# Two fills of idle matmuls in an attention kernel's head, made in row tiles of the TensorE array

## The chip, the cores and the metric

The kernel runs on one core of a Trainium2 chip. A time is the device time of one execution in microseconds; the median over the runs is given. A profile is one execution recorded by the hardware profiler. The engines are TensorE (PE; its weight loads are shown as PEld), VectorE (DVE), ScalarE (ACT), GpSimd (POOL) and SyncE (SP), each with an instruction queue of its own, in order.

## The reference

An attention through 32 inducing points, and then a max-out layer on its result:

```python
def mab(q, kv):
    s = scale * (q @ kv.transpose(0, 2, 1))
    s = s - s.max(-1, keepdims=True)
    a = np.exp(s)
    a /= a.sum(-1, keepdims=True) + 1e-09
    return a @ kv
h = mab(I, x)          # I: (4, 32, 128), x: (4, 12544, 128)
y = mab(x, h)          # (4, 12544, 128), then seen as 50176 rows

g = np.maximum(y @ w1, y @ w2)     # w1, w2: (128, 1024)
return (g @ w_out)                 # w_out: (1024, 128)
```

All inputs and the output are float32; the kernel computes in float16 with float32 sums.

## The kernel before

The core's work falls into a head and a main part. The four batches of x have 98 blocks of 128 rows each. The head computes `h` for batch 0. The main part makes the outputs of all four batches, and beside them, spread out, `h` of the next batch.

**The order.** Each engine's instructions are written out by the program in a fixed order. A planner (`Clock`, `ck` in the code) keeps an estimated time for TensorE, ScalarE, VectorE and each of the eight banks of PSUM. `ck.run(us, mode)` moves TensorE's clock on, with an extra for a change of mode: "full" (the whole 128 x 128 array), "col" (four column tiles of 32 columns) or "row" (four row tiles of 32 rows). `ck.bank[i]` is the time at which bank i has been read out. `bank()` takes the bank with the lowest time, or the one that `only` names. These clocks choose banks, engines and order when the program is built. On the chip the engines wait for each other by semaphores, which follow from what is read and written: an instruction that writes a bank waits until the last reader of what was in it is done.

**The head.** Batch 0 comes in 11 parts, `parts[0]`, four of 14 blocks and then smaller ones. For each part TensorE

- transposes its blocks (`p1_transpose`, L232) into two banks, the first 8 of 14 into one and 6 into the other; VectorE copies the first to SBUF (L236), ScalarE the second (L239),
- accumulates the part before it (`p1_accum`): sums of the exponentials (L271) and `h` (L280), which take the result of ScalarE's exponential (L257),
- computes the scores of the part (`p1_scores`, L248) from the copied transposes into another bank, which ScalarE's exponential (L257) reads.

Two of the eight banks are kept for the accumulation of the whole head (`st[0]["hps"]`, `st[0]["eps"]`; their time is `INF`), so six are in turn.

Between these steps there are idle matmuls: `WARM` = 9 of 512 columns at the start (L665), two in the middle of part 0's transposes, and after the transposes of parts 0, 1 and 2 a `fill` of 2, 2 and 1 matmuls of 512 columns (L657). They multiply `warm`, a tile of zeros, into a bank that nobody reads. For i = 1 and 2 the step of the loop reads: transposes of part i, fill, accumulation of part i - 1, scores of part i.

**The main part.** In turns, TensorE makes phases in row tiles (L990, four units side by side, each with a bank of its own) and full matmuls against `w_out` (L809); ScalarE (L1006) and VectorE (L1009) read the phases' banks. A table `DEV` holds, by the number of the step, where the order departs from the planner's own rule. `pool_accum` (L364) works in column tiles.

Of the kernel before, what the change touches and what calls it, by code (L numbers as in the profile page):

```python
# [102 lines left out]
def kernel(  # L103
# [9 lines left out]
    nc = tc.nc  # L113
# [25 lines left out]
    ck = Clock()  # L139
    uid = [0]  # L140

    def bank(shape, dtype=F32, only=None):
        i = min(range(8), key=lambda j: ck.bank[j]) if only is None else only
        uid[0] += 1
        return i, psum.tile(shape, dtype, name=f"ps{uid[0]}", tag=f"bank{i}", bufs=1)
# [34 lines left out]
    warm = consts.tile([128, 512], F16, name="warm")  # L180
# [16 lines left out]
    with tc.manual_schedule(engines={ET.PE, ET.DVE, ET.Activation, ET.Pool, ET.SP}):  # L197
# [25 lines left out]
        def p1_transpose(b, i, between=0):  # L223
            k0, n = parts[b][i]
            xn = xn_at[b, i]
            h = min(8, (n + 2) // 2)
            for g, m in ((0, h), (h, n - h)):
                if g and between:
                    fill(between)
                bi, ps = bank([128, 8, 128], F16)  # L230
                for j in range(m):
                    nc.tensor.transpose(ps[:, j, :], xn[:, g + j, :], identity16)  # L232
                end = ck.run(0.056 * m, ready=ck.bank[bi], why="T")
                dst = xT_tiles[b % 2][:, k0 + g : k0 + g + m, :]
                if g == 0:
                    nc.vector.tensor_copy(out=dst, in_=ps[:, 0:m, :])  # L236
                    ck.bank[bi] = ck.on_dve(end, 0.08 + 0.075 * m)
                else:
                    nc.scalar.copy(out=dst, in_=ps[:, 0:m, :])  # L239
                    ck.bank[bi] = ck.on_act(end, 0.05 + 0.12 * m)  # L240
                st[b]["xT", i] = max(ck.bank[bi], st[b].get(("xT", i), 0.0))

        def p1_scores(b, i):
            k0, n = parts[b][i]
            bi, ps = bank([128, 512])
            ck.wait(max(ck.bank[bi], st[b].get(("xT", i), 0.0)), "p1")
            for j in range(n):
                nc.tensor.matmul(  # L248
                    out=ps[:, j * M : (j + 1) * M],
                    lhsT=xT_tiles[b % 2][:, k0 + j, :],  # L250
                    rhs=inducingT,
                    start=True,
                    stop=True,
                )
            end = ck.run(0.029 * n)
            et = etp.tile([128, P1, M], F16, name=f"et_{b}_{i}", tag="et")
            nc.scalar.activation(out=et[:, 0:n, :], in_=ps[:, 0 : n * M], func=AF.Exp, scale=scale)  # L257
            ck.bank[bi] = ck.on_act(end, 0.05 + n * M / 1200.0)
            st[b]["et", i] = et, ck.bank[bi]

        def p1_accum(b, i, lo=0, hi=P1):
            k0, n = parts[b][i]
            et, ready = st[b]["et", i]
            hi = min(hi, n)
            xn = xn_at[b, i]
            if b == 0:
                last = i == len(parts[0]) - 1
                ck.wait(ready, "p1")
                for j in range(lo, hi, 4):
                    m = min(4, hi - j)  # L270
                    nc.tensor.matmul(  # L271
                        out=st[0]["eps"][0 : m * M, 0:1],
                        lhsT=et[:, j : j + m, :].rearrange("p k m -> p (k m)"),
                        rhs=ones16[:, 0:1],
                        start=(i == 0 and j == 0),
                        stop=(last and j + m == n),
                        skip_group_check=True,
                    )
                for j in range(lo, hi):
                    nc.tensor.matmul(  # L280
                        out=st[0]["hps"][:, 0:M],
                        lhsT=xn[:, j, :],
                        rhs=et[:, j, :],
                        start=(i == 0 and j == 0),
                        stop=(last and j == n - 1),
                    )
                st[0]["end"] = ck.run(0.029 * (hi - lo) + 0.03 * ((hi - lo + 3) // 4))
                return
# [365 lines left out]
        def fill(n):  # L654
            bi, ps = bank([128, 512])
            for _ in range(n):
                nc.tensor.matmul(out=ps, lhsT=warm[:, 0:128], rhs=warm, start=True, stop=True)  # L657
            ck.run(0.22 * n)
# [4 lines left out]
        bi, ps = bank([128, 512])  # L663
        for _ in range(WARM):
            nc.tensor.matmul(out=ps, lhsT=warm[:, 0:128], rhs=warm, start=True, stop=True)  # L665
        for n in ("h", "e"):
            st[0][n + "b"], st[0][n + "ps"] = bank([128, 512])
            ck.bank[st[0][n + "b"]] = INF
        for i in range(4):
            p1_transpose(0, i, 2 if i == 0 else 0)  # L670
            if i < 3:
                fill(2 - i // 2)
            if i == 0:
                bi, ps = bank([128, 512])
                nc.tensor.transpose(ps[:, 0:M], ind_sb, identity32[0:M, 0:M])
                nc.vector.tensor_copy(out=inducingT, in_=ps[:, 0:M])
                ck.bank[bi] = 0.0
                nc.vector.reduce_sum(out=diag, in_=identity32.rearrange("p (k m) -> p m k", m=M), axis=AX.X)
                for dst, f in ((rep32, DOWN / scale), (repd, 1.0)):
                    nc.vector.tensor_scalar(  # L680
                        out=dst.rearrange("p (k m) -> p k m", m=M),
                        in0=diag[:, None, :].broadcast_to((128, 4, M)),
                        scalar1=f,
                        scalar2=None,
                        op0=ALU.mult,
                    )
            if i > 0:
                p1_accum(0, i - 1)
            p1_scores(0, i)
# [515 lines left out]
```

## Time and profile before

| | us |
|---|---|
| median of 2 runs | 327.43 |
| lowest and highest run | 327.39, 327.47 |
| span of the profiled execution, first to last instruction | 325.6 |
| TensorE busy in the span | 319.8 |
| VectorE busy | 283.1 |
| ScalarE busy | 281.7 |
| GpSimd busy | 25.6 |

The profiled execution has the span of 325.6 us, and some 1.8 us of the run's time lie outside it. Busy times of different engines overlap. The costliest groups are the full matmuls of the main part (L809: 3136 of 128 columns, 217.3 us busy, with overlaps between one and the next) and its phases (L990: 88.7 and 38.8 us). In views of the timeline a line gives the start, the length from the first instruction's start to the last one's end, the engine, the kernel's line, the operation, out<-in, the shape, and how many instructions were put together. A matmul of 128 columns is shown some 0.22 us long although the next one starts 0.056 us after it, because the matmuls are pipelined.

### The profile page before, as it was taken

The page shows a single profiled execution, that of the slowest core. Times are in us where ns is not written, and L with a number is a line of the kernel's source. Part 1 is how long each engine was busy: PE and PEld are TensorE (multiplying, and loading weights), DVE is VectorE, ACT ScalarE, POOL GpSimd, SP SyncE. Part 2 cuts the span into 40 slices and gives each one's busy share as a digit, 9 for nine tenths or more (in the row PEclk, how much of TensorE's full clock was granted, in tenths as well). Part 3 has the DMA queues.
Part 4 walks back from the last instruction along what each step waited for, and adds up shares of the span by engine and source line. Part 5 has one row for each costly group of instructions (what it writes and reads, how often), then busy time and mean ns, then how long its engine had stood idle before and what let it go on. Part 6 is the DMA issues. An engine that isn't in the chain of part 4 may idle for free.

```text
span 325.6 us, 12570 instructions
## 1 busy us (share of the span) xinstructions
PE 319.8 (98%) x5404; PEld 243.0 (75%) x5404; DVE 283.1 (87%) x509; ACT 281.7 (87%) x560; POOL 25.6 (8%) x51
## 2 busy tenths in 40 slices
PE   7999999999999999999999999999999999999996
PEld 3876777777767777777777777777777777778785
DVE  3359989989989998998989999998989999999973
ACT  3679899999989899998888999989969999999961
POOL 7452030000040000000040000000000000000000
PEclk9999999999999999999999999999999999999999
DMA  8999999976279999993389999992312312222233
GB/s 204 208 206 214 286 246 212 172 207 134 97 150 245 225 248 209 201 203 86 116 162 243 214 234 232 190 192 86 115 66 101 113 68 98 90 108 99 85 115 112
DMA packets 70823, 53.65 MB, mean 165 GB/s; under 512 B 52176, under 2 KB 55408, under 8 KB 70768
## 3 DMA queue, kind: packets, MB, share of 16 engines
q1 hardware_dynamic: 64656, 38.63, 49.2%
q0 software_dynamic: 6112, 14.22, 22.3%
q8 instruction: 42, 0.69, 0.9%
q14 instruction: 13, 0.11, 0.1%
HBM read 28.33 MB, written 25.69 MB: 166 GB/s over the span
## 4 chain that ended last, share of the span: by engine, by line
PE 95%; DVE 1%; DMA 1%; ACT 0%; issue 0%; ACTq 0%; DVEq 0%
PE ps L809 61%; PE ps L990 22%; PE ps L591 2%; PE ps L232 2%; PE ps L308 2%; PE ps L364 1%; DMA xf<-in_x_dram 1%; PE ps L248 1%; DVE relu L1009 1%; PE ps L280 1%; PE ps L641 1%; PE ps L766 1%; PE ps L271 1%; PE ps L657 0%; PE ps L473 0%; PE ps L409 0%
## 5 line engine op out<-in xcount | busy, mean ns | idle before, releaser
L1006 ACT ACTIVATE relu<-ps 128x512 f16<-128x512 f32 x461 | 244.8, 602 | 26.6 <-PE ps L990 18.1
L1009 DVE TENSOR_SCALAR relu<-ps 128x512 f16<-128x512 f32 x323 | 206.8, 682 | 16.9 <-PE ps L990 15.3
L809 PE MATMUL ps<-woutp,relu 128*128 128x128 f16 x3136 | 217.3, 220 | 0.0
L809 PEld LDWEIGHTS <-relu 128*128 128x128 f16 x3136 | 176.7, 98 | 39.6 <-issue 29.1
L990 PE MATMUL ps<-e,hwd 32*128 32x512 f16 (+2 forms) x880 | 88.7, 360 | 0.0
L836 DVE TENSOR_TENSOR o<-ps,rp 128x512 f32<-128x512 f32 (+3 forms) x108 | 68.5, 634 | 5.5 <-PE ps L809 3.4
L990 PEld LDWEIGHTS <-hwd 32*128 32x128 f16 x880 | 24.9, 91 | 21.1 <-issue 1.0
L990 PE MATMUL ps<-m,e 32*128 32x128 f16 x381 | 38.8, 217 | 0.0
L990 PEld LDWEIGHTS <-e 32*128 32x128 f16 x381 | 21.3, 93 | 2.6
L165 POOL DMA_DIRECT2D xn<-in_x_dram x31 | 17.0, 557 | 8.2 <-DMA xn<-in_x_dram 4.3
L236 DVE COPY xT<-ps 128x512 f16<-128x512 f16 (+3 forms) x11 | 5.5, 504 | 7.8 <-PE ps L232 7.7
L319 ACT ACTIVATE eu<-ps 128x512 f16<-128x512 f32 x18 | 10.8, 615 | 0.0
L603 ACT ACTIVATE e<-ps 128x512 f16<-128x512 f32 (+2 forms) x21 | 10.5, 577 | 0.0
L164 POOL COPY pace<-hacc 128x1 f32<-128x1 f32 x2 | 0.4, 184 | 114.8 <-DVE hacc L397 114.8
L591 PE MATMUL ps<-xT,hT 128*32 128x512 f16 (+3 forms) x114 | 8.9, 362 | 0.0
L239 ACT COPY xT<-ps 128x768 f16<-128x768 f16 (+3 forms) x11 | 6.1, 556 | 2.7 <-PE ps L232 2.6
L232 PE MATMUL ps<-identity,xn 128*128 128x128 f16 x98 | 7.4, 219 | 0.4 <-DVE xn L661 0.3
L232 PEld LDWEIGHTS <-xn 128*128 128x128 f16 x98 | 5.6, 97 | 1.6 <-DVE xn L661 1.1
L257 ACT ACTIVATE et<-ps 128x448 f16<-128x448 f32 (+4 forms) x11 | 4.5, 413 | 2.6 <-PE ps L248 2.6
L308 PE MATMUL ps<-xT,inducingT 128*32 128x512 f16 x72 | 6.5, 385 | 0.0
L591 PEld LDWEIGHTS <-hT 128*32 128x32 f16 x114 | 3.3, 94 | 4.1 <-issue 3.0
L364 PE MATMUL ps<-xn,eT 128*32 128x128 f16 x288 | 5.5, 220 | 0.0
(96 smaller groups left out, 108.2 us busy)
## 6 DMA issues: line engine op xcount, KB each, us to landing
out_dram<-o SPq DMA_DIRECT2D x90, 256.0 KB, 2.4
xn<-in_x_dram POOLq DMA_DIRECT2D x24, 448.0 KB, 11.8
out_dram<-o SPq DMA_DIRECT2D x10, 128.0 KB, 3.0
xn<-in_moe_w_dram POOLq DMA_DIRECT2D x4, 256.0 KB, 14.1
xn<-in_x_dram POOLq DMA_DIRECT2D x4, 224.0 KB, 10.2
xT<-xn SPq DMA_TRANSPOSE x42, 4.3
xf<-in_x_dram SPq DMA_DIRECT2D x1, 512.0 KB, 3.9
xf<-in_x_dram SPq DMA_DIRECT2D x1, 384.0 KB, 4.3
```

The lines of the kernel that those rows point to most:

```text
L165: nc.gpsimd.dma_start(out=xn_at[b, i][:, 0:n, :], in_=xr[b, :, k0 : k0 + n, :])
L232: nc.tensor.transpose(ps[:, j, :], xn[:, g + j, :], identity16)
L308: nc.tensor.matmul(out=ps[32 * g : 32 * (g + 1), :], lhsT=inducingT, rhs=xT_tiles[b % 2][:, U * u + 4 * g : U * u + 4 * (g + 1), :], start ...
L319: nc.scalar.activation(out=eu, in_=ps, func=AF.Exp, scale=scale, accum_out=st[b]["es"][:, u : u + 1])
L364: nc.tensor.matmul(out=ps[32 * g : 32 * (g + 1), 0:128], lhsT=eT[:, j, 32 * g : 32 * (g + 1)], rhs=xn_of(b, U * v + 4 * g + j), start=(j = ...
L591: nc.tensor.matmul(out=ps[32 * q : 32 * (q + 1), 128 * t : 128 * (t + n)], lhsT=hq, rhs=xT[:, c : c + n, :], start=True, stop=True, tile_p ...
L603: nc.scalar.activation(out=blk.e2[:, 0 : 128 * wd], in_=ps[:, 0 : 128 * wd], func=AF.Exp, scale=st[0]["rs"] if blk.b == 0 else scale,)
L809: nc.tensor.matmul(out=g.ps[:, 128 * c : 128 * (c + 1)], lhsT=g.blk.relu[q][:, 128 * (jb * w4 + t) : 128 * (jb * w4 + t + 1)], rhs=woutp[: ...
L836: nc.vector.tensor_mul(osb[:, 0:n, :], g.ps[:, 0 : n * C].rearrange("p (s c) -> p s c", s=n), rp)
L990: nc.tensor.matmul(**seq[i])
L1006: nc.scalar.activation(out=dst, in_=src, func=AF.Relu)
L1009: nc.vector.tensor_scalar(out=dst, in0=src, scalar1=0.0, scalar2=None, op0=ALU.max)
```

## The change

The fills after the transposes of parts 1 and 2 are made by a new function, `fill_rows`. The fill of part 0 stays.

`fill_rows(i)` sorts the banks by their times, takes a tile in each of the first six, and tells the planner to wait for all six. Its matmuls have 32 rows of `warm` as weights and 32 rows as data, at row tile r (rows 32r to 32r + 31), and write all 128 partitions of a bank.

- For i = 1 there are 20 rounds of four matmuls of 128 columns, row tile r into the r-th of the six banks.
- For i = 2 there are four segments. In each, a row tile has one bank, in four pieces of 128 columns; a tile marked "w4" or "w5" makes one matmul of 512 columns in the fifth or sixth bank instead. Between segments the banks go to other row tiles. Before the third segment stands an empty instruction of TensorE that waits for the last narrow matmul of the first, and before the fourth segment one that waits for the last of the second.

In all these are 80 matmuls for i = 1 and 48 for i = 2 (13, 13, 9 and 13), in place of two and one. The planner is told 1.1 and 0.8 us of mode "row".

```diff
+        marks = {}
+        NOFUSE = False
+
+        def fill_rows(i):
+            order = sorted(range(8), key=lambda j: ck.bank[j])[0:6]
+            ps6 = [bank([128, 512], only=bi)[1] for bi in order]
+            for bi in order:
+                ck.wait(ck.bank[bi], "fill")
+
+            def mm(r, k, lo, n, first):
+                rows = slice(32 * r, 32 * (r + 1))
+                return nc.tensor.matmul(
+                    out=ps6[k][:, lo : lo + n],
+                    lhsT=warm[rows, 0:128],
+                    rhs=warm[rows, 0:n],
+                    start=first,
+                    stop=True,
+                    tile_position=(32 * r, 0),
+                    skip_group_check=True,
+                )
+
+            if i == 1:
+                for v in range(20):
+                    for r in range(4):
+                        mm(r, r, 128 * (v % 4), 128, v == 0)
+            else:
+                seen = set()
+                for n, seg in enumerate(({0: 0, 1: 1, 2: 2, 3: "w4"}, {0: "w5", 1: 1, 2: 2, 3: 3}, {1: "w4", 2: 2, 3: 0}, {0: 1, 1: 3, 2: 2, 3: "w5"})):
+                    for v in range(4):
+                        for r, k in seg.items():
+                            if v == 0 and r == min(seg) and n > 1:
+                                nop = nc.tensor.nop(nofuse=NOFUSE)
+                                tc.add_manual_dep(
+                                    nop.ins,
+                                    marks[n - 2].ins.name,
+                                    mybir.DependencyInfo(mybir.DependencyClass.Sync, mybir.DependencyReason.DATA),
+                                    reason="row tiles of one bank",
+                                )
+                            if isinstance(k, int):
+                                ins = mm(r, k, 128 * v, 128, k not in seen and not seen.add(k))
+                                marks[n] = ins
+                            elif v == 0:
+                                mm(r, int(k[1]), 0, 512, True)
+            ck.run(1.1 if i == 1 else 0.8, "row")
+
         for i in range(4):
             p1_transpose(0, i, 2 if i == 0 else 0)
             if i < 3:
-                fill(2 - i // 2)
+                fill_rows(i) if i else fill(2)
             if i == 0:
```

## The prediction

> **What bounds the kernel now.** I read the page first (busy shares, clock), then the waits of TensorE alone, then the timeline of the head, where the two fills lie, and last a few phases further on, for the price of row tiles.
>
> ```profile
> span 325.6 us, 12570 instructions
> PE 319.8 (98%) x5404; PEld 243.0 (75%) x5404; DVE 283.1 (87%) x509; ACT 281.7 (87%) x560; POOL 25.6 (8%) x51
> PEclk9999999999999999999999999999999999999999
> ```
>
> TensorE is busy for 98% of the span, and no slice shows a clock below nine tenths. The windows of 5 to 24 us and of 24 to 326 us say it more exactly: granted clock 1.00 in both, TensorE busy for 17.79 of 19.00 and 298.20 of 302.00 us. There is no cold stretch that more filling could cure.
>
> ```profile
> engine line waited for: us in total, times, longest us
> PE ps L665 <- DVE warm L213: 1.2, 1, 1.2
> PE ps L232 <- DVE xn L661: 0.3, 1, 0.3
> PE ps L271 <- ACT et L257: 0.3, 1, 0.3
> PE ps L248 <- DVE inducingT L676: 0.3, 1, 0.3
> ```
>
> These are all the waits of TensorE's matmuls in the whole run. None is for a transfer; the last, that of L271, ends at 15.41 us (timeline), and from 20 us on the list is empty. So what delays TensorE in the head delays everything behind it, one for one: no later wait is there to swallow it.
>
> ```profile
> 8.37 0.94 PE L232 MATMUL ps<-identity,xn 128*128 128x128 f16 x14
> 9.14 0.60 PE L657 MATMUL ps<-warm 128*128 128x512 f16 x2
> 9.58 0.34 PE L271 MATMUL ps<-ones,et 128*128 128x1 f16 x4
> ...
> 10.56 0.94 PE L232 MATMUL ps<-identity,xn 128*128 128x128 f16 x14
> 10.75 0.54 ACT L257 ACTIVATE et<-ps 128x448 f16<-128x448 f32 x1 [0.60 <-PE ps L248]
> 11.21 0.69 DVE L236 COPY xT<-ps 128x1024 f16<-128x1024 f16 x1 [1.50 <-PE ps L232]
> ...
> 11.34 0.38 PE L657 MATMUL ps<-warm 128*128 128x512 f16 x1
> ...
> 11.54 0.80 ACT L239 COPY xT<-ps 128x768 f16<-128x768 f16 x1 [0.25 <-PE ps L232]
> 11.56 0.34 PE L271 MATMUL ps<-ones,et 128*128 128x1 f16 x4
> ```
>
> Columns: start, length, engine, line. The chunk loop runs on TensorE without a hole here: transposes (L232), fill (L657), sums (L271), accumulation (L280), scores (L248), transposes again. The fill after chunk 1 holds TensorE from 9.14 to 9.58, 0.44 us; that after chunk 2 from 11.34 to 11.56, 0.22 us.
>
> **The order of the rest does not change.** The planner's clock is told 1.1 and 0.8 us of row work, two changes of mode each, and to wait for all banks. By its own arithmetic TensorE ends chunks 1, 2, 3 at 5.10, 7.43, 9.76 before and at 6.93, 10.80, 13.13 after. At the end of chunk 3 ScalarE (10.38 to 13.75) and VectorE (8.76 to 12.12) are later by the same 3.37, and so is every bank that is still to matter. All its later choices compare differences of these clocks, so the same instructions follow in the same order, in the same banks. What is left is the real time of two fills.
>
> **Prices.** Row tiles of the phases:
>
> ```profile
> 33.93 0.39 PE L990 MATMUL ps<-e,hwd 32*128 32x512 f16 x4
> 34.26 0.90 PE L809 MATMUL ps<-woutp,relu 128*128 128x128 f16 x13
> 35.09 0.23 PE L990 MATMUL ps<-m,e 32*128 32x128 f16 x1
> ...
> 77.15 1.08 PE L364 MATMUL ps<-xn,eT 128*32 128x128 f16 x64
> ```
>
> Four 512-wide matmuls of four row tiles need 0.39 us together, as one does (385 ns in the groups): they run side by side. From their start to the first full matmul is 0.33; the columns take 0.22 of it (one fill of 512: 11.34 to 11.56), so a turn from row to full costs some 0.11. The 13 full matmuls end their columns at 34.26 + 13 x 0.056 = 34.99, and the phase starts at 35.09: 0.10 for full to row. I take 0.10 for each turn, four in all.
>
> [...]
>
> Pace of narrow matmuls, four tiles at once: no row here has four row tiles of 128 columns in a long run. The nearest is L364, four column tiles of 128 columns: (1.08 - 0.22) / 63 = 13.7 ns each, 55 ns for a round of four. The full array's 128 columns take 0.056 (14 transposes from 8.37 to 9.14). I take 0.056 a round. The other bound is the 25 ns of a full-array pair of load and matmul (L248: 14 in 0.35 us), should loads of 128 columns of weights go in one by one.
>
> **Fill 1** (after chunk 1): 20 rounds of four. It uses the four longest-free banks; the latest is that of chunk 0's scores, read by ScalarE's L257 from 8.55 to 9.09, over before 9.14. So it waits for nothing, and takes 0.10 + 20 x 0.056 + 0.10 = 1.32 us where 0.44 was: **+0.88**.
>
> **Fill 2** (after chunk 2): four segments of four rounds, 0.224 each. It takes all six free banks, the two latest as spares "w4" and "w5". These are the banks of chunk 2's own transposes, just written and still to be copied out by VectorE (L236) and ScalarE (L239). In the times of the trace of before: row work may start at 11.34 + 0.10 = 11.44. Its fourth matmul writes w4, so it waits for VectorE's copy, 11.21 + 0.69 = 11.90, and some 0.05 for the signal (ScalarE's copy of chunk 3 ends at 14.35 on the chain of waits, and TensorE goes on at 14.39). The second segment begins with w5 and waits for ScalarE's copy, 11.54 + 0.80 + 0.05 = 12.39. The first segment is over by then (11.95 + 0.224). Three segments and a turn remain: 12.39 + 3 x 0.224 + 0.10 = 13.16, where L271 began at 11.56: **+1.60**. These two waits are new. Behind them in TensorE's order stand the rest of the fill, the accumulation of chunk 1, the scores of chunk 2 and the whole head; ScalarE and VectorE wait for those. Nothing covers it, because the copies used to run beside accumulation (L280), which now comes later.
>
> **TensorE's waits on itself:** before segment 3 for a matmul of segment 1, before segment 4 for one of segment 2. The first is long past. The second ends with the last round of segment 2, started at 12.39 + 0.17, 0.22 long, plus 0.05: 12.83, just where segment 3's columns end (12.84). I take 0. Below nothing is excluded, for the wait replaces none; above, I allow 0.2 each, the longest idle time put down to issue before L990's loads.
>
> Sum: 0.88 + 1.60 = 2.48 us. The profiled execution's span of 325.6 plus 1.8 outside it is the 327.43 of the median. **Forecast: 327.43 + 2.48 = 329.9 us, 0.76% slower.** A change under 2% is about what a measurement of this kernel cannot tell from none, so this counts as the same.
>
> Low end: if the copies were over in time, fill 2 would cost 0.10 + 0.90 + 0.10 - 0.22 = 0.88 and the sum be 1.76; with 0.4 less, a tenth of the 3.8 us that TensorE is idle from 24 to 326 us, should those holes move, 328.8. High end: at 25 ns a matmul fill 1 takes 80 x 0.025 = 2.0 (0.88 more) and a segment of 13 0.33 (three of them 0.3 more): 3.66, or 331.1, and half of a self-wait's 0.2 makes it 331.2.
>
> **Rivals.**
> *The fills are hidden (0.08).* If the loads of x set the head's pace, longer fills would only take the place of waiting, and the time stay at 327.4 to 328.2. For it: the transfers are dense in the head (share 1.17 from 5 to 24 us). Against: TensorE waits for no transfer, in the list above.
>
> *Row tiles do not run side by side (0.04).* If 128-wide row matmuls went one at a time, at 56 ns, fill 1 would take 4.5 us instead of 1.12 (+3.4). Segments two and four of fill 2, 12 x 0.056 + 0.22 = 0.89, would cost 0.67 more each, the third (nine matmuls) 0.44, and the first, no longer over in its wait, 0.45. Together 5.6 on top of 2.48: 335.5 us, 2.5% slower. It decides once the extra passes 4.1 us, at about 48 ns a matmul. Against: the phases' four in 0.39.
>
> *The clock falls (0.04).* Cold fills (L665) take 3.85 / 9 = 0.43 us where warm ones take 0.22. To pass 2% the head would need 8.1 us more of work at half pace. Against: 1.00 throughout, across a stop of 0.3 us; the longest new one, for VectorE's copy, is 0.5.
>
> [...]
>
> *A faster kernel (0.02)* would need 6.5 us; all of TensorE's waits after warming sum to 0.9, so I see no source.
>
> **How the numbers follow.** My forecast has the remaining 0.82. The range, 328.8 to 331.2, takes in its ends, and leaves the rivals and a little of its own tails out. Faster by over 2%: 0.02; slower by over 2%: 0.05 (serial tiles, or most of a cold clock); within: 0.93.
>
> **What would show it.** Right: the first L271 after fill 1 some 0.88 us later than 9.58, that after fill 2 2.5 us later than 11.56; about 80 row matmuls in 1.1 us; a stop of 0.4 to 0.5 us in fill 2 put down to VectorE's L236 and a shorter one to ScalarE's L239; the rest of the head and of the span shifted by the same 2.5 us. Wrong: L271 on time, a clock below 1.00, row matmuls over 14 ns apart, or a main part whose length differs by more than 0.5 us.

## The result, and the profile after

| | before | the change |
|---|---|---|
| median, us | 327.43 (2 runs) | 332.93 (2 runs, 332.69 and 333.16) |
| ratio, 95% interval | | 1.016 [1.0123, 1.0197] |
| span of the profiled execution, us | 325.6 | 331.0 |
| granted clock, mean over the span | 1.000 | 0.995 |

The kernel became 5.5 us slower; 2.5 were forecast, with 331.2 as the end of the range. Beside thirteen other runs of the kernel before (median 327.52) four later runs of the change gave 333.33, ratio 1.0177 [1.0158, 1.0196].

From the page of the profile after, the lines that answer to those of before:

```profile
span 331.0 us, 12820 instructions
PE 324.1 (98%) x5529; PEld 246.3 (74%) x5529; DVE 283.0 (85%) x509; ACT 281.9 (85%) x560; POOL 25.5 (8%) x51
PEclk9979999999999999999999999999999999999999
```

VectorE and ScalarE do what they did. The clock line has a digit that was not there: 7 in the third slice, 16.6 to 24.8 us.

The waits of TensorE's matmuls:

```profile
PE ps L665 <- DVE warm L213: 1.2, 1, 1.2
PE ps L680 <- issue: 1.1, 1, 1.1
PE ps L248 <- DVE inducingT L721: 0.3, 1, 0.3
PE ps L680 <- DVE xT L236: 0.3, 1, 0.3
PE ps L469 <- PE ps L591: 0.3, 1, 0.3
```

L680 is the matmul of `fill_rows`. The wait for VectorE's copy was forecast. The second of the list was not: 1.1 us for "issue", that is, for nothing that the profile shows. (The last is at 28.35 us, and will come up again.) The timeline of TensorE says where:

```profile
9.92 1.30 PE L680 MATMUL ps<-warm 32*128 32x128 f16 x80
11.15 0.35 PE L271 MATMUL ps<-ones,et 128*128 128x1 f16 x4
...
13.02 0.23 PE L680 MATMUL ps<-warm 32*128 32x128 f16 x3
13.53 1.37 PE L680 MATMUL ps<-warm 32*128 32x512 f16 x38 [0.28 <-DVE xT L236]
15.96 0.34 PE L680 MATMUL ps<-warm 32*128 32x128 f16 x7 [1.06 <-issue]
16.23 0.35 PE L271 MATMUL ps<-ones,et 128*128 128x1 f16 x4
...
17.22 1.58 PE L232 MATMUL ps<-identity,xn 128*128 128x128 f16 x14
```

Fill 1 goes as forecast. Fill 2 stops in the middle of its fourth segment, six matmuls behind its last wait on itself. The sixth begins at 14.57 and the seventh at 15.96; less 0.05 for the sixth one's columns, that is a stop of 1.33 us. Then the transposes of part 3 take 1.58 us where they took 0.94: the clock has fallen. The windows show it (second column: length, then busy times of PE, PEld, DVE, ACT, POOL; behind them PEclk):

```profile
13.92:17.33 3.41, 2.30 (x69) 1.80 (x69) 0.00 (x0) 0.00 (x0) 1.97 (x3) 1.00 1.14 203
17.33:20.75 3.42, 3.42 (x56) 3.08 (x52) 0.94 (x2) 1.89 (x3) 2.12 (x4) 0.50 1.19 205
20.75:24.16 3.41, 3.39 (x85) 3.24 (x85) 1.45 (x4) 2.40 (x7) 1.27 (x3) 1.00 1.38 208
```

In the clock's own records it is at half from 17.33 to 20.75 us.

**Where 5.4 us between the two profiles come from**, by the starts of the same steps: the first scores (L248) 8.02 to 8.70, 0.68 before the change begins; L271 behind fill 1 9.58 to 11.15, 0.89 more; L271 behind fill 2 11.56 to 16.23, 3.10 more, of which 1.33 is the stop and 1.77 the fill; the transposes of part 4 14.56 to 19.88, 0.65 more, the slow window; the first phase 24.29 to 29.65, 0.04 more, and 5.4 at the end. The main part is as long as it was. The first 0.68 is chance: the clock came up later at the start of this execution (the two matmuls of L657 that need 0.60 us took 1.06 at 6.05). By the clock's records of eleven profiles it comes up between 3.8 and 7.1 us, in before's at 4.75 and in after's at 7.09; the kernel before itself ran from 327.0 to 328.4 us in 27 later runs.

### The profile page after: what moved, and what is told of

Same layout as the page of the kernel before. It is cut to its first block, busy times and chain, and to the rows that moved or that the text cites. A ratio compares the mean times of both kernels' runs of the same rounds, so it can differ in the third digit from the quotient of the medians.

```text
span 331.0 us, 12820 instructions
## 1 busy us (share of the span) xinstructions
PE 324.1 (98%) x5529; PEld 246.3 (74%) x5529; DVE 283.0 (85%) x509; ACT 281.9 (85%) x560; POOL 25.5 (8%) x51
## 4 chain that ended last, share of the span: by engine, by line
PE 97%; DVE 1%; issue 1%; ACT 0%; DVEq 0%; ACTq 0%
PE ps L854 60%; PE ps L1035 22%; PE ps L232 2%; PE ps L591 2%; PE ps L308 2%; PE ps L364 1%; PE ps L665 1%; PE ps L280 1%; PE ps L248 1%; DVE relu L1054 1%; PE ps L641 1%; PE ps L680 1%; PE ps L271 1%; PE ps L811 1%; PE ps L473 0%
## 5 line engine op out<-in xcount | busy, mean ns | idle before, releaser
L1035 PEld LDWEIGHTS <-hwd 32*128 32x128 f16 x880 | 24.8, 91 | 21.1 <-issue 1.0
L257 ACT ACTIVATE et<-ps 128x448 f16<-128x448 f32 (+4 forms) x11 | 4.5, 413 | 6.6 <-PE ps L248 6.6
L232 PE MATMUL ps<-identity,xn 128*128 128x128 f16 x98 | 8.8, 244 | 0.1
L591 PE MATMUL ps<-xT,hT 128*32 128x512 f16 (+3 forms) x114 | 8.5, 362 | 0.0
L232 PEld LDWEIGHTS <-xn 128*128 128x128 f16 x98 | 6.8, 110 | 1.7 <-DVE xn L661 0.9
L591 PEld LDWEIGHTS <-hT 128*32 128x32 f16 x114 | 3.2, 94 | 3.9 <-issue 2.8
```

What stands on the lines that cost most here:

```text
L591: nc.tensor.matmul(out=ps[32 * q : 32 * (q + 1), 128 * t : 128 * (t + n)], lhsT=hq, rhs=xT[:, c : c + n, :], start=True, stop=True, tile_p ...
L1035: nc.tensor.matmul(**seq[i])
```

## The experiments

Two theories for the stop. **A:** TensorE ran out of instructions. In the trace exactly 446 weight loads and matmuls of TensorE begin before the stop, and the instruction queue (q8) brings its first packet, of 16 KB, at 13.72 us. Before, the 446th came at 16.62 us, with a packet at 14.10. The row fills put 250 more into TensorE's list (11,058 loads and matmuls after 10,808), and the queue has one packet more. Its line on the page of before, and then of after (packets, MB, share of 16 engines):

```profile
q8 instruction: 42, 0.69, 0.9%
```

```profile
q8 instruction: 43, 0.70, 0.9%
```

**B:** the second fill makes the stop itself, by its handing over of banks between row tiles and its waits of TensorE on itself.

All ran beside the kernel before (medians 327.63, 327.52 and 327.70 in the three sets). In every variant the planner is told the same as by the kernel that it was made from.

**1. The first fill alone.**

```diff
-                fill_rows(i) if i else fill(2)
+                fill_rows(i) if i == 1 else fill(2 - i // 2)
```

> Only the first fill in row tiles, the second as before. Theory A (instructions run out): TensorE's first 446 loads and matmuls are there at the start, the next 256 become usable 5.5 us after the 190th has begun; the 446th now falls into the transposes of part 3, so TensorE stops there for about 1.5 us, and the kernel is 0.9 + 1.5 = 2.4 us slower than before, 3 us if the clock falls for a window. Theory B (the stop of 1.3 us belongs to the second fill, its handing over of banks and its waits of TensorE on itself): no stop, 0.9 us slower.

Measured: 331.28 us, ratio 1.0116 [1.0098, 1.0134], 3.65 us slower. TensorE's timeline:

```profile
13.35 0.61 PE L232 MATMUL ps<-identity,xn 128*128 128x128 f16 x8
15.99 0.51 PE L232 MATMUL ps<-identity,xn 128*128 128x128 f16 x6 [2.04 <-issue]
```

There is no second fill, and TensorE stops all the same, behind its 446th load or matmul, in the middle of part 3's transposes; and the clock falls for one window (mean 0.993 to 0.995 in the four runs). That is A. The size of the stop was off, 2.2 us and not 1.5: the packet began at 13.68 and the next instruction 2.3 us later, 6.35 us behind the 190th (9.64) and not 5.5, as I had worked out from two runs.

**2. The second fill alone.**

```diff
-                fill_rows(i) if i else fill(2)
+                fill_rows(i) if i == 2 else fill(2 - i // 2)
```

> Only the second fill in row tiles, the first as before. Theory A: the 446th load or matmul comes at about 15.8 us, the next instructions are usable at 16.3: a stop of about 0.5 us, and not in the fill but behind it (in part 3); 1.7 + 0.5 = 2.2 us slower than before. Theory B: the stop of 1.3 us stays in the fill's fourth segment; 1.7 + 1.3 = 3.0 us slower. Either way 0.7 more if a window of the clock falls below its share.

Measured: 330.08 us, 1.0085 [1.0055, 1.0115], 2.45 us slower. The fill has no stop, with its hand-over and its waits on itself all there, so B fails here. Of A's 0.5 us half came, and where A put it: the 447th follows the 446th (16.07) after 0.29 us, at 16.35, and the profile puts the wait of its load down to issue:

```profile
16.35 0.24 PEld L248 LDWEIGHTS <-xT 128*128 128x128 f16 x7 [0.21 <-issue]
```

This is the eighth of 14 loads of part 3's scores. In run 3, TensorE stops behind the eighth for ScalarE's copy; here that copy ended at 16.26, so the short stop cost next to nothing. A stop of 0.7 us came at the 702nd (446 + 256). One of the four runs (330.99 us) has a mean clock of 0.995, the others 0.998 to 1.000.

**3. Both fills in few, wide matmuls, each row tile with its own bank.**

```diff
-                for v in range(20):
-                    for r in range(4):
-                        mm(r, r, 128 * (v % 4), 128, v == 0)
...
+            for v in range(5 if i == 1 else 4):
+                for r in range(4):
+                    mm(r, r, 0, 512, True)
```

> Both fills in four row tiles, with matmuls of 512 columns (20 and 16 in place of 80 and 48), each row tile with a bank of its own, no spares, no waits of TensorE on itself; the same time of row work. Theory A: the 446th instruction comes 0.8 us or more after the next ones are there: no stop. Both theories: 0.88 + 0.88 = 1.8 us slower than before, clock 1.00 from the first warm window on.

Measured: 329.02 us, 1.0045 [1.0028, 1.0063], 1.4 us slower. The 446th comes at 16.47; the 447th, at 16.98, waits for ScalarE's exponential (L257) and not for issue. Clock 1.00 (0.998 in one run).

**4. The first fill of the change, a second fill with nothing handed over.**

```diff
+            for v in range(20 if i == 1 else 16):
+                for r in range(4):
+                    mm(r, r, 128 * (v % 4), 128, v == 0)
```

> First fill as in the change; second fill of 64 matmuls of 128 columns, each row tile with a bank of its own: no spares, so no wait for the copies, no bank handed over, no wait of TensorE on itself. Theory A: the 446th instruction is reached sooner, in the middle of the second fill, and the stop grows from 1.3 to about 2.3 us: 0.9 + 0.9 + 2.3 = 4.1 us slower than before, about 4.8 with a fallen clock; as slow as the change or nearly. Theory B: no stop, 1.8 us slower.

Measured: 333.49 us, 1.0181 [1.0163, 1.0199], 5.9 us slower. TensorE's timeline:

```profile
12.93 0.78 PE L680 MATMUL ps<-warm 32*128 32x128 f16 x41
15.85 0.51 PE L680 MATMUL ps<-warm 32*128 32x128 f16 x23 [2.14 <-issue]
```

With every wait of the second fill taken away the stop grew, to 2.30 us: TensorE gets to its 446th load or matmul sooner, at 13.50 us, where the change got there at 14.57, and stops there until 15.84 (15.95 in the change). B is out. Here too 446 loads and matmuls come first. The time is 1.1 us above what A forecast with a fallen clock. In the profiled run the first scores are 0.59 us late before any fill, as the clock came up later (6.75 us), and a further stop, of 0.5 us, comes at the 958th (446 + 512).

**5. A stop and nothing else.** In the kernel before, the fill after part 2 waits for two writes by VectorE; no row tile, no instruction more on TensorE.

```diff
-            if i < 3:
+            if i == 2:
+                gate = outp.tile([128, 4, C], F32, name="gate", tag="o")
+                nc.vector.memset(gate, 0.0)
+                nc.vector.memset(gate, 0.0)
+                bi, ps = bank([128, 512])
+                nc.tensor.matmul(out=ps, lhsT=gate[:, 0, :].bitcast(F16)[:, 0:128], rhs=warm, start=True, stop=True)
+                ck.run(0.22)
+            elif i < 3:
                 fill(2 - i // 2)
```

> The kernel before, with one stop of TensorE put in: the fill after part 2 is one full matmul that waits for two writes of 512 columns by VectorE (begun behind its copy of part 2); no row tiles, no instruction more on TensorE. The stop is about 1.7 us (11.3 to 13.0 us). If the clock follows the share of a window of 3.41 us in which columns stream (below some 0.4: half clock in the next window, as three runs so far would have it), the window with the stop falls to 0.25 to 0.35 where it holds the whole stop, and the clock halves for one window behind it: 1.7 + 0.7 = 2.4 us slower; where two windows share the stop, none falls below and it is 1.7. If the clock fell because of the row tiles, it stays at 1.00 in every run: 1.7.

Measured: 329.52 us, 1.0056 [1.0038, 1.0075], 2.0 us slower. In the profiled run TensorE waits 1.65 us for VectorE, and the clock stays up:

```profile
9.83:13.25 3.42, 2.08 (x48) 1.75 (x46) 1.69 (x4) 2.06 (x3) 1.06 (x2) 1.00 1.09 208
```

Two of the four runs have a mean clock of 0.995, as one window of 3.41 us at half would make it (0.5 x 3.41 / 327.7 = 0.005 less), and take 329.61 and 329.94 us; the two near 1.00 take 328.67 and 329.43. So a stop alone can bring the clock down, without row tiles; these two runs were not profiled, so where their slow window lies isn't on record, but the 27 later runs of the kernel before and the ten of run 6 all have 0.999 or 1.000. My rule for when, a share of the window, does not hold: this window has TensorE busy for 2.08 us and kept the clock, that of the change before the fall (13.92 to 17.33) has 2.30 and lost it.

**6. No fills after parts 1 and 2**, in the kernel before.

```diff
-            if i < 3:
-                fill(2 - i // 2)
+            if i == 0:
+                fill(2)
+            elif i < 3:
+                bank([128, 512])
+                ck.run(0.22 * (2 - i // 2))
```

> The kernel before without the fills after parts 1 and 2. If they lie on the path, it is up to 0.6 us faster; what the copies and the next instructions (446th usable at 16.4 us, 702nd at about 22.6 us) hold back is not gained: I expect 0 to 0.4 us faster. If they are needed to keep the clock, a window falls below 0.4 and it is 0.3 to 0.7 us slower. Theory A has it that TensorE stops longer at the 702nd load or matmul than the 0.3 us of the kernel before.

Measured: 327.23 us (10 runs), 0.9993 [0.9983, 1.0002]: no difference that can be told. The clock is 0.999 or 1.000 in all ten, so it does not need these fills. The longer stop at the 702nd that A had forecast did not come: the 703rd follows after 0.32 us, but between these two steps (L591 and L469) that is the distance in run 9 too, away from any such number.

**7. The change's hand-over and waits, with wide matmuls.**

```diff
+                for n, seg in enumerate(({0: 0, 1: 1, 2: 2, 3: 4}, {0: 5, 1: 1, 2: 2, 3: 3}, {1: 4, 2: 2, 3: 0}, {0: 1, 1: 3, 2: 2, 3: 5})):
+                    for r, k in seg.items():
...
+                        marks[n] = mm(r, k, 0, 512, True)
```

> The change with every four matmuls of 128 columns made one of 512: the first fill 20, the second 16, still with the two spares, the banks handed from row tile to row tile, and the two waits of TensorE on itself. Against the run with own banks (1.4 us slower than before) it prices the waits for the copies and the handing over: 0.8 to 0.9 more, 2.3 us slower than before in all. Theory A: no stop at the 446th instruction, clock 1.00. Theory B (handing over makes the stop and then the clock fall): 1.3 us and more on top, 3.6 or slower.

Measured: 330.11 us, 1.0077 [1.0062, 1.0092], 2.6 us slower, no stop at the 446th, clock 0.998 to 1.000. Against run 3 the spares and the hand-over cost 1.2 us in the medians, where 0.8 to 0.9 were expected; in the two profiles, from the first scores to L271 behind fill 2, it is 0.77 (6.03 and 5.26).

**8. The change again.**

> The change once more, beside the same runs of the kernel before: 5.2 us slower, a stop in front of the 447th load or matmul of TensorE, usable 2.0 to 2.1 us after the instruction queue's first packet of 16 KB begins, and one window at half clock behind it.

Measured: 333.33 us, 5.8 slower than the runs beside it. The profiled execution stopped for 1.69 us behind the 446th, until 15.96, which is 2.4 us after the packet began (13.55); the expectation's 2.0 to 2.1 went by packet times that were 0.24 us late against the timeline. The clock stayed at half for three windows of 3.41 us, not one, with TensorE busy but for the end of the stop (PEclk is the third number from the end):

```profile
15.58:18.99 3.41, 3.03 (x54) 2.81 (x55) 0.47 (x1) 0.54 (x1) 2.90 (x5) 0.50 1.18 206
18.99:22.41 3.42, 3.42 (x66) 3.05 (x64) 0.67 (x3) 1.82 (x3) 1.65 (x4) 0.50 1.40 201
22.41:25.82 3.41, 3.41 (x64) 3.41 (x62) 1.29 (x4) 2.21 (x6) 1.07 (x2) 0.50 1.11 218
```

The four runs lie in the order of their clocks: 332.70 us at 0.995, 333.31 and 333.35 at 0.990, 334.06 at 0.985, by an estimate from those means one, two, two and three slow windows (0.5 x 3.41 / 331 = 0.005 each; the profile of the 334.06 shows three): some 0.7 us each.

**9. The change with its first fill alone made wide**, 20 matmuls in place of 80; the second untouched.

```diff
-                for v in range(20):
-                    for r in range(4):
-                        mm(r, r, 128 * (v % 4), 128, v == 0)
+                for v in range(5):
+                    for r in range(4):
+                        mm(r, r, 0, 512, True)
```

> The change with its first fill alone in matmuls of 512 columns: 20 in place of 80 in the same 1.1 us of row work; the second fill is the change's own, narrow, handed over, with its two waits. Theory A: 120 loads and matmuls fewer in front of the second fill, so the 446th comes behind the fill, at about 16 us, when the next ones are usable (15.6 to 16.4 us): a stop of 0 to 0.4 us, and the clock falls seldom; 2.6 to 3.0 us slower than before, where the change is 5.5 to 5.8 slower. Theory B: the second fill is as it was, so the stop of 1.3 us stays in its fourth segment and the clock falls behind it: 4.5 us slower or more.

Measured: 329.75 us, 1.0075 [1.0051, 1.0099], 2.05 us slower, less than the 2.6 to 3.0 of A and far from the 4.5 of B; clock 0.998 to 1.000. TensorE's timeline:

```profile
9.11 1.26 PE L680 MATMUL ps<-warm 32*128 32x512 f16 x20
10.30 0.35 PE L271 MATMUL ps<-ones,et 128*128 128x1 f16 x4
...
12.17 0.23 PE L680 MATMUL ps<-warm 32*128 32x128 f16 x3
12.68 1.37 PE L680 MATMUL ps<-warm 32*128 32x512 f16 x45 [0.28 <-DVE xT L236]
13.98 0.35 PE L271 MATMUL ps<-ones,et 128*128 128x1 f16 x4
```

The same second fill, with the same waits, now runs through, and 3.8 of the 5.8 us of run 8 are gone, by taking 120 instructions out of the first fill without shortening it.

The profiles together, by the records of TensorE's loads and matmuls and of the instruction queue (us; the packet is the first of 16 KB):

```
                      packet begins   446th begins   447th begins
before                    14.10          16.62          16.62
the change                13.72          14.57          15.95
1 first alone             13.68          13.74          15.99
2 second alone            14.02          16.07          16.35
3 both wide               13.61          16.47          16.98
4 nothing handed over     13.54          13.50          15.84
5 a stop alone            14.21          18.83          18.83
6 no fills                13.59          16.45          16.45
7 handed over, wide       13.27          17.80          17.81
8 the change again        13.55          14.22          15.96
9 first wide              12.94          16.11          16.11
```

Where TensorE got to the 447th early (the change, 1, 4, 8, and by a little 2), it went on 2.2 to 2.4 us after the packet's begin, whatever stood there: a fill, a transpose or a score. In no profile did the 447th begin sooner than that after the packet. Where the 446th came later, there is no stop for issue.

## Why the prediction was wrong

**What held.** The order of the main part was the same and a delay in the head went through to the end (5.32 us at part 4, 5.36 at the first phase, 5.4 at the end). Row tiles run side by side: 80 matmuls in 1.30 us. Fill 1 was priced at +0.88 and measured 0.89. Fill 2's two waits came at the forecast places: moved on by the 1.57 us of delay before it, w4 was due at 13.52 and came at 13.53, w5 at 13.96 and came at 13.97. From its first matmul to L271 fill 2 was to take 1.72 us and took 1.81 (run 9). Runs 9 and 7, which differ from the change by instructions saved, are 2.05 and 2.6 us slower than before; the forecast of 2.48 lies in both intervals.

**The step that failed** is the sum "0.88 + 1.60 = 2.48 us". It priced the 128 matmuls by the time that their columns take and gave no price to their number. The row fills bring TensorE sooner to its 446th load or matmul, at 14.57 us where it was at 16.62 before, and the 447th began at 15.95, 2.2 us after the packet did (13.72). Runs 1, 4 and 9 show that this term alone makes the stop: it is there without the second fill (2.2 us), larger without the hand-over (2.30), and gone with 120 instructions fewer. In the change's two profiles it is 1.33 and 1.69 us.

**The clock.** The rival "the clock falls" was given 0.04, against it "across a stop of 0.3 us; the longest new one, for VectorE's copy, is 0.5". The stop to come was not 0.5 but 1.3 to 2.3 us, and the clock fell in all twelve runs of 1, 4 and 8 (mean 0.985 to 0.995), in the profiled ones at the end of the window that holds the stop or most of it. In run 5 a stop alone went with it in two of four runs, so row tiles are not needed. It cost about 0.7 us a window (run 8). The rival was right as a mechanism and wrong in its price, for it was made to stand for 8 us of half pace only.

**By terms**, from medians: fills as forecast 2.0 to 2.6 (runs 9, 7), the stop 1.3 to 1.7, one to three slow windows at 0.7; together 4.0 to 6.4, against 5.5 and 5.8 measured.

**Smaller slips.** The prediction says that a change under 2% can hardly be told from none; the intervals here are 0.1 to 0.4% wide to each side, and 1.6% is clear of them. In the high end, the remaining segments at 25 ns a matmul have 13, 9 and 13 matmuls, so they are 0.2 us longer and not 0.3. In the rival of serial row tiles, the first segment has three matmuls in front of its wait, which makes its 0.45 some 0.28. Nothing above hangs on these.

The first stop comes behind 446 loads and matmuls and lasts up to 2.3 us. Smaller stops lie 256 and 512 further on: at the 702nd (446 + 256) in the kernel before, 0.3 us (L591 at 22.34 took 0.71 where the next took 0.40), and at the 958th in the change (L469 at 28.35, 0.35 us later behind L591 than in run 9).

In the change's two profiles the slow stretch is one and three times 3.41 us long (17.33 to 20.75, and 15.58 to 25.82 in run 8). In the first the clock came down behind a stop of 1.33 us, in a window (13.92 to 17.33) that was busy before and after it.

**Open.** That TensorE runs out of instructions is read from where the stops lie and when the packets begin (the first at 13.72 us in the change, 2.2 us before the 447th); no view shows how many it holds. When a packet begins is explained in part. In the eleven profiles the second packet begins 2.6 to 3.7 us after the 447th load or matmul, wherever that lies (15.84 to 18.83 us), and the first 2.0 to 4.0 us after the 191st, 256 earlier (9.64 to 11.19 us). So it looks as if the next packet is asked for each time 256 instructions have been used; no run tried that by itself. What sets those 2.0 to 4.0 us is not known. The transfers are dense there (share 1.05 to 1.16), which may hold the packet back; that was not tried. Why the clock falls behind one stop and not behind another is open too: in run 5 the mean is 0.995 in two runs and 0.999 and 1.000 in the others. No version beat the kernel before; run 6 equals it.

## What to carry to other kernels

Count instructions as well as columns. In this dense head of short matmuls TensorE stopped for 1.3 to 2.3 us (the change, runs 1, 4 and 8), most likely out of instructions, and the stop shows as "issue" without a releaser, behind the same 446th load or matmul in each of them. To fill time on TensorE, use few wide matmuls (512 columns), in row tiles too: the same row work with 120 instructions fewer was some 3.8 us faster (run 9 against run 8, each by its own runs of before). Before adding filler to keep the clock up, take the existing filler out once: here, without the fills after parts 1 and 2, the clock was 0.999 or 1.000 in all ten runs and the time 327.23 us against 327.52 (run 6).

## What the runs showed that was not expected

The kernel before already lived at the edge: its 446th instruction came 0.2 us after the time at which the 447th could have gone on (by an estimate from the 2.2 to 2.4 us of the profiles with the stop 14.10 + 2.3, against 16.62), and it did stop at the 702nd, for 0.3 us. And a core whose clock had fallen needed three windows to get it back in the profile of run 8 (15.58 to 25.82 us), with TensorE busy for 3.03 us of the first and throughout the other two.
